# Softmax sums inverted by a GpSimd power, maximum taken by VectorE from a bfloat16 copy, and a new issue order, in a state-space and sliding-attention kernel

## Chip, cores and metric

One Trainium2 chip, one core. The metric is the device time of one execution in microseconds (us), the median of several runs of the same kernel. The engines are named as in the profile: PE (TensorE, matmuls; PEld its weight loads), DVE (VectorE), ACT (ScalarE), POOL (GpSimd) and SP (SyncE, which issues most DMAs).

## The reference

The inputs and the output are bfloat16. Part A is a diagonal state-space layer with L = 2048 steps, 448 channels and 448 complex states; part B is attention with 16 heads of 28, in which each position looks at 8 positions, 2 apart. Cut to what matters:

```python
# A
Lam_bar = exp(dt * Lam);  B_bar = ((Lam_bar - 1) / Lam)[:, None] * Bmat
h = Lam_bar * h + (x @ B_bar.T)[t]            # for each of 2048 steps
y = 2.0 * (h @ Cmat.T).real + x * Dskip
# B
q, k, v = split(x @ wqkv)                     # 16 heads of 28
logits[s, w] = (q[s] . k[s - 2 * w]) * scale  # w = 0..7; -1e9 where s - 2 * w < 0
attn = softmax(logits, axis=w)
o[s] = sum_w attn[s, w] * v[s - 2 * w]
b = o @ wo
out = concatenate([y, b], -1)                 # (1, 2048, 896)
```

The change is in the softmax of part B: the maximum over the 8 positions, the exponentials, their sum, and the product with the sum's reciprocal.

## The kernel before, in words

**Order.** Every piece of work is a unit of the `Planner` (L112), with an engine, a booked cost and dependences. The list `ORDER` (L51) holds all 685 unit numbers in the order in which they are issued; every engine executes its own in that order, so an instruction that waits holds up all behind it on its engine. What the units acquire and release (PSUM banks, the three `prods` buffers) fits that order.

**Part B.** The 2048 positions lie as 128 chunks on the partitions by 16 offsets, and the work is done in two halves of 8 offsets, b = 1 and then b = 0. For each half:

- `qk` (L584): DVE multiplies q with the shifted k (products `prods`, L654, L656, L660). PE sums them over the head's elements into the PSUM tile `logits`, 128 x 8 x 128 float32 (L672, L678). DVE can go on to the next product once one of three buffers is free.
- `softmax` (L695): PE adds the mask (L290); DVE takes the maximum over the 8 positions by a reduction out of PSUM (L701, `mx`); PE subtracts it (L705); ACT takes the exponentials (L711, `ex_sb`); PE sums the 8 positions into `sm_ps` (L716); DVE takes the reciprocal (L720, `rsum`) and multiplies (L722, `attn_t`); a transposing DMA that SP issues (L727) brings the result to `attn`.
- `v_proj` (L736): PE projects v (L753, L760), ACT evicts it (L218) into `vd`; POOL zeroes the halo (L778) and SP copies it (L773, L774).
- `pv` (L786): for each of the four groups of 4 offsets, DVE multiplies `attn` with v four times (L819, 128x3584 each) and adds three times (L822) and once over half the width (L838). In the last group the last add is made in two halves (L841). Three groups are transposed by a DMA (L872), the last by PE (L884); PE multiplies with wo (L900, L908, L915), ACT evicts, SP stores (L925).

**Part A** runs beside it. PE computes the inputs of the states (L1247) and the scan as products with tables of powers of `Lam_bar`, which DVE builds (L1197, `pw`, one for each of 7 blocks of states), with ACT evicting between the steps (L1263 to L1364). C is transposed by a DMA (L1024, `Ccat`), and the outputs are matmuls (L1458, L1462), evicted by ACT (L218) or, at the end, by DVE (L1474) and stored (L1477). `load_skip` (L1420) loads Dskip and A's x again for the last outputs, and DVE multiplies them (L1439).

Of the kernel before, what the change touches and what calls it, by code (L numbers as in the profile page):

```python
# [25 lines left out]
W = 8  # L26
# [13 lines left out]
NC = 3  # L40
# [6 lines left out]
ADD = (0, 0, 0, 0, 0, 0, 0)  # L47
EADD = (0, 0, 0, 0)
# [160 lines left out]
class Ctx:  # L209
# [111 lines left out]
class PartB:  # L321
# [373 lines left out]
    def softmax(self, b, prio):  # L695
        nc, pool, V, P, cx = self.nc, self.pool, self.nc.vector, self.plan, self.cx
        box = {}

        def top():
            box["mx"] = pool.tile([NCH, NCH], bf16, name="mx", tag="mx")  # L700
            V.tensor_reduce(box["mx"][:], self.lg[b][:].rearrange("p w q -> p q w"), axis=AX.X, op=ALU.max)  # L701
# [15 lines left out]

        def norm():
            r = pool.tile([NCH, 1, NCH], f32, name="rsum", tag="rs")
            V.reciprocal(r[:, 0, :], box["sm"][:])  # L720
            box["a"] = pool.tile([NCH, W, NCH], bf16, name="attn_t", tag="at_t")
            V.tensor_tensor(box["a"][:].rearrange("p w (c a) -> p w c a", c=2), box["e"][:].rearrange("p w (a c) -> p w c a", c=2),  # L722
                            r[:].rearrange("p o (a c) -> p o c a", c=2).to_broadcast([NCH, W, 2, 64]), op=ALU.mult)
# [5 lines left out]
        u = P.add("DVE", 1.23, top, [u], prio, acq="mx")  # L729
# [3 lines left out]
        u = P.add("DVE", 2.175, norm, [u], prio, rel=("s", "ex"), acq="at")  # L733
# [52 lines left out]
    def pv(self, b, prio, deps):  # L786
# [13 lines left out]
        lasts, halves, trs = {}, {}, {}  # L800
        for r in (1, 0):
            last = getattr(self, "pv_last", None)
            half = getattr(self, "u_half", None)
            ahead = half is not None
            us = (5, 4, 1, 0)
            for n in range(4):

                def step(n=n, r=r, part=0, half=half):
# [14 lines left out]
                    if n == 0:  # L823
                        mul(1 if half else 0)
                        mul(2 if half else 1)
                    elif n == 1 and half:
                        mul(3)
                        mul(0)
                    elif n == 2 and half:
                        add(1)  # L830
                        add(2)
# [3 lines left out]
                    elif 2 * b + r > 0:  # L835
                        add(3)
                        if not EADD[2 * b + r]:
                            V.tensor_tensor(acc[:, n1:2 * n1], acc[:, 0:n1], acc[:, n1:2 * n1], op=ALU.add)  # L838
# [4 lines left out]
                for u in us[:2 + ahead] if n == 0 else us[n + 1 + ahead:n + 2 + ahead] if n < 3 else ():  # L843
# [3 lines left out]
                cost = 2 * vec2(2 * n1) if n < 3 else vec2(2 * n1) + vec2(n1) * (not EADD[2 * b + r]) if 2 * b + r > 0 else vec2(n1)  # L847
                last = P.add("DVE", cost, step, dd + [self.u_attn[b], last, *self.u_prod[0], *self.u_prod[1], *self.u_lg[0], *self.u_lg[1],
                                         *self.u_vm, *self.u_proj, *deps, half if n == 1 else None], prio - 0.1 * r)
# [5 lines left out]
            g = 2 * b + r  # L855
            halves[g] = self.u_half = None
            if EADD[g]:

                def merge(g=g):
                    acc = self.acc[g]  # L860
                    nc.gpsimd.dma_start(acc[:, n1:2 * n1], acc[:, 0:n1], accum_op=ALU.add)
                halves[g] = self.u_half = P.add("POOL", 1.1, merge, [last], PRI["wo"], lat=3.5)
# [736 lines left out]
```

## Time and profile before

| | |
|---|---|
| median of 3 runs | 139.99 us (139.88 to 140.03) |
| the profiled execution's own time | 140.0 us |
| its span on the engines | 138.3 us |
| mean granted clock of PE | 0.997 |
| busy: PE, DVE | 131.3 us (95%), 123.0 us (89%) |
| busy: ACT, POOL | 88.3 us (64%), 17.7 us (13%) |
| the softmax's maximum on DVE (L701), 2 times | 1.22 us each |
| the reciprocal on DVE (L720), 2 times | 0.95 us each |
| the multiply behind it (L722), 2 times | 1.23 us each |

In a timeline a row holds the start in us, the duration in us, the engine, the line, the operation, the tiles (output <- inputs) with their shapes and types, and a count of instructions; in brackets stands how long the engine sat idle ahead of it and which instruction ended that. In a group, the numbers are the total busy time in us and the mean of one in ns. PE's matmuls are pipelined, so their durations overlap. L-numbers are lines of the kernel.

### The profile page before, as it was taken

The numbers are of one execution on the slowest core, as the hardware profiler recorded it, in microseconds if no ns is written. First come the engines' busy times: TensorE is split into PE (matmuls) and PEld (weight loads), VectorE is DVE, ScalarE is ACT, GpSimd is POOL, SyncE is SP. The second block draws the span as 40 slices with busy tenths as digits, with TensorE's granted clock in tenths as the row PEclk, the third lists the DMA queues.
The fourth block names the chain that finished last, engine by engine and source line by source line (L and its number), as shares of the span: only waits on it lengthen the run. The fifth ranks groups of instructions, "written<-read, shape, count | busy, mean of one in ns | idle before, by whom it ended". The sixth has DMA issues, their size and how long they took to land.

```text
span 138.3 us, 2835 instructions
## 1 busy us (share of the span) xinstructions
PE 131.3 (95%) x1065; PEld 67.2 (49%) x1071; DVE 123.0 (89%) x134; ACT 88.3 (64%) x199; POOL 17.7 (13%) x69
## 2 busy tenths in 40 slices
PE   7999989999999999999999999999999999999790
PEld 2534334444455453656534563556565455445450
DVE  1369998899999999997999999999999999999920
ACT  3555587998554976657695998689547151721571
POOL 7589830025000000000000000000000000000000
PEclk9999999999999999999999999999999999999998
DMA  4968965658658525648899039350093425575163
GB/s 128 269 126 208 179 87 61 153 130 95 81 113 53 97 52 112 179 104 131 167 222 198 0 67 240 95 111 0 0 95 103 139 78 118 141 163 169 35 197 100
DMA packets 41694, 16.58 MB, mean 120 GB/s; under 512 B 33685, under 2 KB 41044, under 8 KB 41681
## 3 DMA queue, kind: packets, MB, share of 16 engines
q1 hardware_dynamic: 41618, 16.40, 57.6%
q8 instruction: 8, 0.13, 0.4%
q14 instruction: 5, 0.04, 0.1%
q10 hardware_dynamic: 63, 0.01, 0.0%
HBM read 4.32 MB, written 3.67 MB: 58 GB/s over the span
## 4 chain that ended last, share of the span: by engine, by line
DVE 39%; PE 38%; SPq 9%; issue 5%; ACT 3%; DMA 3%; DVEq 0%; ACTq 0%
DVE rb L822 11%; DVE prods L819 11%; SPq L366 6%; PE v_ps L760 6%; PE scb L1247 5%; DVE rb L819 4%; PE scp L1247 4%; PE logits L672 3%; DMA rb<-in_B_x_dram 3%; DVE pw L1197 2%; PE qk_ps L481 2%; DVE prods L656 2%; PE wo_ps L915 2%; DVE rb L838 2%; ACT qk L218 1%
## 5 line engine op out<-in xcount | busy, mean ns | idle before, releaser
L819 DVE TENSOR_TENSOR prods<-attn,vd 128x3584 bf16<-128x3584 bf16 x12 | 24.0, 2018 | 0.0
L822 DVE TENSOR_TENSOR rb<-rb,prods 128x3584 bf16<-128x3584 bf16 x11 | 22.2, 2019 | 0.1
L656 DVE TENSOR_TENSOR prods<-qk 128x3072 bf16<-128x3072 bf16 (+1 forms) x15 | 19.1, 1325 | 0.0
L481 PE MATMUL qk_ps<-rb 128*128 128x512 bf16 x60 | 14.4, 379 | 0.7 <-DMA rb<-in_B_x_dram 0.6
L1462 PE MATMUL y_ps<-Ccat,qk 128*128 128x448 bf16 x60 | 14.6, 352 | 0.0
L218 ACT CAST vd<-v_ps 128x448 bf16<-128x448 f32 x16 | 7.9, 540 | 5.2 <-PE v_ps L760 4.9
L1247 PEld LDWEIGHTS <-Bcat 128*128 128x128 bf16 x84 | 7.5, 100 | 7.4 <-issue 1.1
L1294 ACT CAST ubuf<-scb 128x64 bf16<-128x64 f32 x35 | 7.3, 220 | 5.9 <-PE scb L1301 3.5
L218 ACT CAST qk<-wo_ps 128x448 bf16<-128x448 f32 (+1 forms) x16 | 8.1, 529 | 4.5 <-PE wo_ps L908 2.8
L1462 PE MATMUL y_ps<-Ccat,h 128*128 128x448 bf16 x45 | 11.0, 353 | 0.0
L1247 PE MATMUL scb<-xaT_sb,Bcat 128*128 128x512 bf16 x42 | 10.9, 380 | 0.0
L218 ACT CAST qk<-y_ps 128x448 bf16<-128x448 f32 (+1 forms) x9 | 5.6, 663 | 8.2 <-issue 4.2
L760 PE MATMUL v_ps<-rb 128*128 128x448 bf16 x48 | 10.1, 353 | 0.0
L220 ACT ACTIVATE qk<-qk_ps 64x512 bf16<-64x512 f32 (+1 forms) x15 | 8.9, 599 | 1.7 <-PE qk_ps L488 1.3
L481 PEld LDWEIGHTS <-rb 128*128 128x128 bf16 x60 | 5.6, 98 | 7.8 <-issue 1.0
L660 DVE TENSOR_TENSOR prods<-qk 128x768 bf16<-128x768 bf16 (+3 forms) x18 | 9.1, 566 | 0.1
L1462 PEld LDWEIGHTS <-qk 128*128 128x128 bf16 x60 | 5.8, 98 | 5.3 <-ACT qk L1364 0.2
L819 DVE TENSOR_TENSOR rb<-attn,vd 128x3584 bf16<-128x3584 bf16 x4 | 8.1, 2021 | 0.1
L908 PE MATMUL wo_ps<-wo_p,rb 128*128 128x448 bf16 x36 | 8.1, 353 | 0.0
L1197 DVE TENSOR_TENSOR pw<-Dm,spair 128x1920 bf16<-128x1920 bf16 x7 | 8.1, 1150 | 0.0
L218 ACT CAST qk<-qk_ps 128x512 bf16<-128x512 f32 (+2 forms) x11 | 6.3, 585 | 2.5 <-PE qk_ps L488 1.1
L1247 PE MATMUL scp<-xaT_sb,Bcat 128*128 128x512 bf16 x30 | 7.8, 381 | 0.0
(197 smaller groups left out, 259.0 us busy)
## 6 DMA issues: line engine op xcount, KB each, us to landing
out_dram<-qk SPq DMA_DIRECT2D x32, 112.0 KB, 1.8
vd<-vd SPq DMA_DIRECT2D x3, 392.0 KB, 4.5
rb<-in_B_wqkv_dram SPq DMA_DIRECT2D x3, 336.0 KB, 4.5
qk<-in_A_x_dram SPq DMA_DIRECT2D x1, 448.0 KB
ra<-in_A_B_re_dram SPq DMA_DIRECT2D x1, 392.0 KB, 4.3
ra<-in_A_B_im_dram SPq DMA_DIRECT2D x1, 392.0 KB
rb<-in_A_C_re_dram SPq DMA_DIRECT2D x4, 98.0 KB, 2.9
rb<-in_A_C_im_dram SPq DMA_DIRECT2D x4, 98.0 KB, 3.5
```

What stands on the lines that cost most here:

```text
L218: nc.scalar.copy(out, in_)
L220: nc.scalar.mul(out, in_, scale)
L366: nc.sync.dma_start(self.xT[:, j], bass.AP(x.tensor, x.offset + j * D - DT, [[T * D, NCH], [1, KT * NCH]]), transpose=True)
L481: nc.tensor.matmul(out(n), lhsT=w(n, full, k), rhs=self.xT[:, j:j + 4, k, :], start=(not rfirst and k == 1), stop=(rfirst and k == KT - 1) ...
L656: V.tensor_tensor(out.rearrange("p i j k q -> p i (j k) q"), qq.unsqueeze(1).to_broadcast([NCH, 2, 4 * nk, NCH]), bass.AP(kk.tensor, kk.of ...
L660: V.tensor_tensor(jk(out[:, i, a:e]), qq, kk, op=ALU.mult)
L760: nc.tensor.matmul(box["ps"][:].rearrange("p h d -> p (h d)"), lhsT=self.xT[:, j, k, :], rhs=self.wv[:, k, :], start=False, stop=(k == KT ...
L819: V.tensor_tensor(tmp[i].rearrange("p (j d h) -> p j d h", j=8, d=DH), aa, self.vd[:, o:o + 8], op=ALU.mult)
L822: V.tensor_tensor(acc, acc, tmp[i], op=ALU.add)
L1197: V.tensor_tensor(t[:], self.o["Dm"][:].rearrange("p (a b) -> p a b", b=2).unsqueeze(1).to_broadcast([NCH, 2 * NPW, 32, 2]), self.sp[:, m ...
L1247: mt(box[i], lhsT=self.Bcat[:, k, m, :], rhs=self.xk(slice(i, None, 4), k), start=(i % 2 == 0 and k == 0), stop=False, **kw)
L1462: nc.tensor.matmul(ps, lhsT=h, rhs=self.Ccat[:, m, :], start=(m == 0 and not skip), stop=(m == NM - 1), skip_group_check=True)
```

## The change

In each of the two softmaxes:

- ACT first copies the masked logits out of PSUM into a bfloat16 tile (`low`, L700 of the new kernel). DVE takes the maximum from it by three element-wise maxima over 4, 2 and 1 of the positions (L704, L705, L707: 512, 256 and 128 elements), in place of the one reduction out of PSUM.
- ACT copies the sums out of PSUM into `rsum` (`total`, L726); POOL raises them to the power -1 in place (`rec`, L730), with a tile of -1.0 that it sets at the start (L251) as the second operand; DVE does the multiply alone (L735). The bank of the sums is released by ACT's copy.

That is three more units in each half, 691 in all, and `ORDER` is a new list: through the first five numbers of its eighth row it is the old one with shifted numbers, behind them it is another order. What else the diff shows are options that were all zero, with their code.

```diff
+        self.minus = pool.tile([NCH, 1], f32, name="minus")
+        G.memset(self.minus[:], -1.0)
...
+        def low():
+            box["l"] = pool.tile([NCH, W, NCH], bf16, name="lg_bf", tag="lg_bf")
+            nc.scalar.copy(box["l"][:], self.lg[b][:])
+
         def top():
+            t = box["l"]
+            V.tensor_tensor(t[:, 0:4], t[:, 0:4], t[:, 4:8], op=ALU.max)
+            V.tensor_tensor(t[:, 0:2], t[:, 0:2], t[:, 2:4], op=ALU.max)
             box["mx"] = pool.tile([NCH, NCH], bf16, name="mx", tag="mx")
-            V.tensor_reduce(box["mx"][:], self.lg[b][:].rearrange("p w q -> p q w"), axis=AX.X, op=ALU.max)
+            V.tensor_tensor(box["mx"][:], t[:, 0], t[:, 1], op=ALU.max)
...
+        def total():
+            box["r"] = pool.tile([NCH, 1, NCH], f32, name="rsum", tag="rs")
+            nc.scalar.copy(box["r"][:, 0, :], box["sm"][:])
+
+        def rec():
+            r = box["r"][:, 0, :]
+            nc.gpsimd.tensor_tensor(r, r, cx.minus[:].to_broadcast([NCH, NCH]), op=ALU.pow)
+
         def norm():
-            r = pool.tile([NCH, 1, NCH], f32, name="rsum", tag="rs")
-            V.reciprocal(r[:, 0, :], box["sm"][:])
+            r = box["r"]
...
-        u = P.add("DVE", 1.23, top, [u], prio, acq="mx")
+        u = P.add("ACT", act(1024), low, [u], -1)
+        u = P.add("DVE", vec2(512) + vec2(256) + vec2(128), top, [u], prio, acq="mx")
...
-        u = P.add("DVE", 2.175, norm, [u], prio, rel=("s", "ex"), acq="at")
+        u = P.add("ACT", act(128), total, [u], -1, rel="s")
+        u = P.add("POOL", 2.0, rec, [u], -1)
+        u = P.add("DVE", 1.23, norm, [u], prio, rel="ex", acq="at")
```

DVE, from just ahead of the first softmax's reciprocal (b = 1) to the beginning of the weighted products, before (`prods<-qk` are products of q and k, `pw` is a table of powers, `rb<-attn,vd` the first weighted product):

```order
L656 TENSOR_TENSOR prods<-qk 128x3072
L720 RECIPROCAL rsum<-sm_ps 128x128
L722 TENSOR_TENSOR attn_t<-ex_sb,rsum 128x1024
L660 TENSOR_TENSOR prods<-qk 128x768 x2
L660 TENSOR_TENSOR prods<-qk 128x1536
L660 TENSOR_TENSOR prods<-qk 128x768 x2
L660 TENSOR_TENSOR prods<-qk 128x1536
L701 TENSOR_REDUCE mx<-logits 128x128
L819 TENSOR_TENSOR rb<-attn_1004,vd 128x3584
L819 TENSOR_TENSOR prods<-attn_1004,vd 128x3584
```

The same place in the new order:

```order
L655 TENSOR_TENSOR prods<-qk 128x3072
L659 TENSOR_TENSOR prods<-qk 128x256 x2
L659 TENSOR_TENSOR prods<-qk 128x512
L1196 TENSOR_TENSOR pw<-Dm,spair 128x1920
L735 TENSOR_TENSOR attn_t<-ex_sb,rsum 128x1024
L704 TENSOR_TENSOR lg_bf<-lg_bf 128x512
L705 TENSOR_TENSOR lg_bf<-lg_bf 128x256
L707 TENSOR_TENSOR mx<-lg_bf 128x128
L1196 TENSOR_TENSOR pw<-Dm,spair 128x1920
L833 TENSOR_TENSOR rb<-attn_1140,vd 128x3584
L833 TENSOR_TENSOR prods<-attn_1140,vd 128x3584 x2
```

The reciprocal is gone, the multiply (L735) stands behind all the products of q and k, and a second table of powers stands between the maximum and the weighted products; before, a table followed the first two of those.

DVE around the second softmax's multiply, which lies inside the second group of weighted products, before:

```order
L819 TENSOR_TENSOR prods<-attn_1004,vd 128x3584
L1197 TENSOR_TENSOR pw<-Dm,spair 128x1920
L720 RECIPROCAL rsum<-sm_ps 128x128
L722 TENSOR_TENSOR attn_t<-ex_sb,rsum 128x1024
L819 TENSOR_TENSOR prods<-attn_1004,vd 128x3584
L822 TENSOR_TENSOR rb<-rb,prods 128x3584
```

And in the new order, where it stands between two groups:

```order
L836 TENSOR_TENSOR rb<-rb,prods 128x3584 x2
L845 TENSOR_TENSOR rb<-rb 128x1792
L1196 TENSOR_TENSOR pw<-Dm,spair 128x1920
L735 TENSOR_TENSOR attn_t<-ex_sb,rsum 128x1024
L833 TENSOR_TENSOR rb<-attn_1140,vd 128x3584
```

The reciprocal is gone here too; the multiply now follows a table of powers behind a half add (L845).

POOL, from the zeroing of the scan's states (`S`) to its last instruction, before:

```order
L1212 MEMSET S 128x7x2
L402 MEMSET wo_p 64x448
L403 MEMSET wo_p 64x448
L778 MEMSET vd 1x896 x3
L778 MEMSET vd 1x448
```

And in the new order:

```order
L1211 MEMSET S 128x7x2
L794 MEMSET vd 1x896
L794 MEMSET vd 1x448
L730 TENSOR_TENSOR rsum<-rsum,minus 128x128
L401 MEMSET wo_p 64x448
L402 MEMSET wo_p 64x448
L794 MEMSET vd 1x896 x2
L730 TENSOR_TENSOR rsum<-rsum,minus 128x128
```

The two powers stand between the zeroings of v's halo (`vd`) and of the padding of wo (`wo_p`).

On SP the same transfers stand in another order: the transposition of C goes behind the second transposition of the weights, and the load of Dskip (L1429 before, L1410 now) moves from among the last stores to just ahead of the transposition of C.

More of the change, by code (lines that the diff above doesn't have):

```diff
@@ L39 @@
 NF = 3
-NC = 3
 WARM = 6
@@ L799, in pv, with step @@
         self.oTd = getattr(self, "oTd", {})
-        lasts, halves, trs = {}, {}, {}
+        lasts, trs = {}, {}
         for r in (1, 0):
             last = getattr(self, "pv_last", None)
-            half = getattr(self, "u_half", None)
-            ahead = half is not None
             us = (5, 4, 1, 0)
             for n in range(4):
-                def step(n=n, r=r, part=0, half=half):
+                def step(n=n, r=r, part=0):
                     alloc()
@@ L823, in step @@
                     if n == 0:
[L824 to L827, printed above, removed]
                         mul(0)
-                    elif n == 2 and half:
-                        add(1)
-                        add(2)
+                        mul(1)
                     elif n < 3:
@@ L836, in step @@
                         add(3)
[L837 to L838 removed]
+                        V.tensor_tensor(acc[:, n1:2 * n1], acc[:, 0:n1], acc[:, n1:2 * n1], op=ALU.add)
                     else:
@@ L842, in pv @@
                 dd = []
-                for u in us[:2 + ahead] if n == 0 else us[n + 1 + ahead:n + 2 + ahead] if n < 3 else ():
+                for u in us[:2] if n == 0 else us[n + 1:n + 2] if n < 3 else ():
                     o = j0 + 4 * r + DIL * u
@@ L846, in pv @@
                         dd += self.u_vh[p] if p < HALO else [self.u_v[p - HALO]]
-                cost = 2 * vec2(2 * n1) if n < 3 else vec2(2 * n1) + vec2(n1) * (not EADD[2 * b + r]) if 2 * b + r > 0 else vec2(n1)
+                cost = 2 * vec2(2 * n1) if n < 3 else vec2(2 * n1) + vec2(n1) if 2 * b + r > 0 else vec2(n1)
                 last = P.add("DVE", cost, step, dd + [self.u_attn[b], last, *self.u_prod[0], *self.u_prod[1], *self.u_lg[0], *self.u_lg[1],
-                                         *self.u_vm, *self.u_proj, *deps, half if n == 1 else None], prio - 0.1 * r)
+                                         *self.u_vm, *self.u_proj, *deps], prio - 0.1 * r)
             lasts[r] = [last, last]
@@ L854, in pv @@
             self.pv_last = last
[L855 to L862, printed above, removed]
             if not hasattr(self, "u_first"):
@@ L872, in trd @@
                     nc.sync.dma_start(t, self.acc[g][:, n1:2 * n1], transpose=True)
-                trs[r] = P.add("SP", 1.7, trd, [halves[g] or lasts[r][1]], PRI["wo"], lat=3.6)
+                trs[r] = P.add("SP", 1.7, trd, [lasts[r][1]], PRI["wo"], lat=3.6)
         for j in range(j0, j0 + JB):
@@ L1314, in ev3, with carry @@
                 nc.scalar.copy(hget()[:, 3, 0:384], box[3][:, 0:384])
-            def carry(out, lt, Sc, hv, new=False):
-                mt(out[:, 0:NCH], lhsT=lt, rhs=Sc, start=new, stop=True, **kw)
+            def carry(out, lt, Sc, hv):
+                mt(out[:, 0:NCH], lhsT=lt, rhs=Sc, start=False, stop=True, **kw)
                 mt(out[:, NCH:512], lhsT=lt, rhs=hv[:, 3, 0:384], start=False, stop=True, **kw)
@@ L1329, in ev1f, with back @@
                 nc.scalar.copy(hget()[:, 1, :], box[1])
-            def again(n, box=box, pair=pair):
+            def back(n, box=box, pair=pair, hget=hget):
                 if pair and n == 0:
@@ L1403, in scan @@
             b0 = b2 = eh
-            add = bool(ADD[m])
-            if not hold[0] and not add:
+            if not hold[0]:
                 b0 = P.add("PE", pe(1, 512), lambda f=back: f(0), [b0], PRI["bk"] + m * 0.1, acq="W" if pair else "s")
-            if not hold[pair ^ 1] and not add:
+            if not hold[pair ^ 1]:
                 b2 = P.add("PE", pe(1, 512), lambda f=back: f(1), [b2, b0], PRI["bk"] + m * 0.1, acq=None if pair else "s")
-            v0 = P.add("PE", pe(2, 256), s6, [b0, u3], pc, acq=("W" if pair else "s", "cP") if add else None)
-            v2 = P.add("PE", pe(1, 512), s7, [b2, u1, v0 if add and pair else None], pc, acq="s" if add and not pair else None)
+            v0 = P.add("PE", pe(2, 256), s6, [b0, u3], pc)
+            v2 = P.add("PE", pe(1, 512), s7, [b2, u1], pc)
             if pair:
@@ L1415, in scan @@
             done[m] = P.add("POOL", 0.0, lambda: None, [w0, w2, u1], rel=("fl", "pw"), lat=0.0)
-            if add:
-                w0 = w2 = P.add("POOL", 1.2, addin, [w0, w2], pc, rel="cP", lat=3.0)
             self.u_h.append((w0, u1, w2, [u3, eh]))
```

32 lines of the change are left out of this document (9 added, 23 removed), and 56 rows, old and new, of the table ORDER.

## The prediction

> **What bounds the kernel now.** I read first how busy the engines are in three stretches of the span: from the first maximum to the first weighted products, the long middle, and the end. The columns are the stretch, its length, then busy time and instructions of PE, PE's weight loads, DVE, ACT and POOL, and the granted clock.
>
> ```profile
> 44.00:65.00 21.00, 20.65 (x243) 11.23 (x243) 20.07 (x25) 14.86 (x36) 0.00 (x0) 1.00 0.56 108
> 65.00:127.00 62.00, 61.65 (x428) 32.79 (x431) 61.59 (x37) 39.38 (x100) 0.00 (x0) 1.00 0.53 119
> 127.00:138.30 11.30, 6.68 (x55) 3.77 (x53) 5.09 (x7) 4.99 (x10) 0.00 (x0) 0.96 0.32 102
> ```
>
> Two engines are full at once. From 44 to 127 us PE is busy 82.3 of 83 us and DVE 81.7. GpSimd does nothing after 44 us, and ScalarE has gaps. So work taken off DVE gains only as far as PE can be brought forward as well, while a delay on either moves the end at once, unless a wait swallows it.
>
> Next, the timeline of DVE through the first softmax (start, duration, instruction, and in brackets the idle time before it), and then through the second.
>
> ```profile
> 44.19 1.23 DVE L701 TENSOR_REDUCE mx<-logits 128x128 bf16<-128x1024 f32 x1
> 45.33 3.42 DVE L656 TENSOR_TENSOR prods<-qk 128x3072 bf16<-128x3072 bf16 x2
> ...
> 56.82 0.95 DVE L720 RECIPROCAL rsum<-sm_ps 128x128 f32<-128x128 f32 x1
> 57.87 1.23 DVE L722 TENSOR_TENSOR attn_t<-ex_sb,rsum 128x1024 bf16<-128x1024 bf16 x1
> 59.02 3.69 DVE L660 TENSOR_TENSOR prods<-qk 128x768 bf16<-128x768 bf16 x6
> 63.51 1.22 DVE L701 TENSOR_REDUCE mx<-logits 128x128 bf16<-128x1024 f32 x1 [0.80 <-PE logits L290]
> 64.65 2.02 DVE L819 TENSOR_TENSOR rb<-attn,vd 128x3584 bf16<-128x3584 bf16 x1
> ```
>
> ```profile
> 86.59 0.95 DVE L720 RECIPROCAL rsum<-sm_ps 128x128 f32<-128x128 f32 x1
> 87.64 1.23 DVE L722 TENSOR_TENSOR attn_t<-ex_sb,rsum 128x1024 bf16<-128x1024 bf16 x1
> 88.78 2.02 DVE L819 TENSOR_TENSOR prods<-attn,vd 128x3584 bf16<-128x3584 bf16 x1
> ```
>
> From start to start a maximum takes 1.14 and a reciprocal 1.05. In both softmaxes the reciprocal stands in an unbroken run of DVE. The only idle time here is the 0.80 before the second maximum, which waits for PE's mask. The attention-weighted products (L819) begin at 64.65, and from there DVE runs on to the halves of the last add.
>
> ```profile
> 126.48 2.09 DVE L841 TENSOR_TENSOR rb<-rb,prods 128x1792 bf16<-128x1792 bf16 x2
> 128.49 1.08 DVE L1439 TENSOR_TENSOR qk<-qk,rb 128x1792 bf16<-128x1792 bf16 x1
> ```
>
> ```profile
> 128.63 0.29 PE L884 MATMUL pt_o<-ident,rb 128*128 128x128 bf16 x2 [0.49 <-DVE rb L841]
> ...
> 130.46 0.92 PE L915 MATMUL wo_ps<-wo_p,rb 128*128 128x448 bf16 x4 [0.52 <-ACT qk L218]
> ...
> 131.98 0.61 PE L884 MATMUL pt_o<-ident,rb 128*128 128x128 bf16 x8 [0.17 <-DVE qk L1474]
> 132.43 2.43 PE L915 MATMUL wo_ps<-wo_p,rb 128*128 128x448 bf16 x12
> ```
>
> The add ends at 128.57, and the span 9.73 later, at 138.3. PE ends at 134.86; the 3.44 behind it are the last eviction, store and close. In the tail PE waits 0.49 + 0.52 + 0.17 = 1.18.
>
> **The maximum.** The reduction over PSUM goes; a ScalarE copy of the logits and three DVE maxima come. The nearest rows are ScalarE's copy of the same shape (and of 128x128, used further down), and DVE's two-input bf16 products of 256 and 512 elements.
>
> ```profile
> L1260 ACT CAST qk<-scP 128x1024 bf16<-128x1024 f32 x2 | 2.1, 1050 | 0.0
> ...
> L1287 ACT CAST eB<-scb 128x128 bf16<-128x128 f32 x7 | 2.0, 279 | 0.4 <-PE scb L1283 0.4
> ```
>
> ```profile
> L660 DVE TENSOR_TENSOR prods<-qk 128x256 bf16<-128x256 bf16 x4 | 1.0, 284 | 0.0
> L660 DVE TENSOR_TENSOR prods<-qk 128x512 bf16<-128x512 bf16 x2 | 0.8, 418 | 0.0
> ```
>
> The three, of 512, 256 and 128 elements, cost 0.42 + 0.28 + 0.21 (the slope between the two rows continued) = 0.91, and between 0.75, if their ends overlap, and 1.1, with a gap behind each; against 1.14 I take −0.25 per softmax. The price is the copy ahead of them, 1.05 and some 0.25 of hand-over, which stands between the mask and the maximum. Where it is hidden depends on when PE comes to the mask.
>
> ```profile
> 43.40 0.20 PE L290 MATMUL logits<-mrow,mcol 128*128 128x4 bf16 x2
> ...
> 63.27 0.21 PE L290 MATMUL logits<-mrow,mcol 128*128 128x4 bf16 x2
> ```
>
> ```profile
> L1247 PE MATMUL scb<-xaT_sb,Bcat 128*128 128x512 bf16 x42 | 10.9, 380 | 0.0
> L760 PE MATMUL v_ps<-rb 128*128 128x448 bf16 x48 | 10.1, 353 | 0.0
> ```
>
> Matmuls overlap: 512 columns follow each other every 0.216 us (0.81 for three, less the 0.38 of the last), 448 columns every 0.19. The new order has seven v matmuls fewer ahead of the first mask, −1.3, of which 0.3 to 0.5 are lost waiting for the sums: mask at about 42.6, copy done at 43.9, before DVE arrives at 44.16. No wait, so −0.25. Ahead of the second mask stand ten 512-column scan matmuls and eight small ones fewer, −1.9; less about 0.5 of waiting, the mask comes at 62.0, the copy is ready at 63.4, and the maxima last until 64.4.
>
> **The reciprocals leave DVE:** −1.05 each. Without any cost of the power, DVE's work from 45.33 to 62.71 (17.38) becomes 16.33 and starts 0.27 sooner: it ends at 61.4. But DVE then waits 2.1 for the copy, where it waited 0.80. The multiply now stands behind all products, and one more power table (L1197, pitch 1.07) stands ahead of the weighted products: 64.4 + 1.07 = 65.45. Before, with that table counted, they would have begun at 65.72. So of 1.6 freed, 0.27 is left at this place. Behind it the second reciprocal gives −1.05 in full, since DVE has no gap there, and a small cast that moved ahead −0.07. Sum so far: **−1.39**, DVE's end at 127.2.
>
> **The transposition of the weights** now starts at the multiply's end.
>
> ```profile
> attn<-attn_t SPq DMA_TRANSPOSE x2, 3.1
> ```
>
> That is 61.4 + 3.15 = 64.6 against 65.45: 0.85 of slack. Its cover is used up if the multiply comes 0.85 later.
>
> **The power.** Each softmax adds a ScalarE copy of 128x128 (0.28 by the row above) and a GpSimd operation, with two hand-overs, ahead of the multiply. No power is in the trace. GpSimd's two-input rows in float32 are these:
>
> ```profile
> L1124 POOL TENSOR_TENSOR cs<-sh 128x210 f32<-128x210 f32 x1 | 0.5, 539 | 0.0
> ...
> L1081 POOL TENSOR_TENSOR karg<-kv,arg 128x105 f32<-128x105 f32 x1 | 0.4, 362 | 0.0
> ```
>
> They give 1.69 ns an element, so 0.40 for 128: the lower bound, if a power costs what a product does. A logarithm, a product and an exponential make several such passes: five make 2.0, ten 4.0, the upper bound. I take 2.0, which is also what the code books for this unit; its bookings have been good where the trace can test them (1.23 for the maximum against 1.22; 2.175 for reciprocal and multiply against 0.95 + 1.23 = 2.18).
>
> Alone, that would be hidden. The first sums are finished on PE at about 57.5, their copy at 58.5, the power runs from 58.65 to 60.65, and the multiply is due at 60.25: it would come 0.4 to 0.6 late, which the 0.85 covers. In the second softmax the sums are finished more than 5 us ahead of the multiply. The question is whether GpSimd and DVE can read side by side at all.
>
> ```profile
> 14.80 1.08 POOL L1129 TENSOR_SCALAR la<-la,turn 128x7 f32<-128x7 f32 x1
> ```
>
> ```profile
> 14.68 0.96 DVE L654 TENSOR_TENSOR prods<-qk 128x1536 bf16<-128x1536 bf16 x1
> ```
>
> This is the one place in the trace where a reading GpSimd instruction meets a two-input product of DVE, and it bears against the change: an operation of 7 elements, whose twin took 0.50, took 1.08 and ended 0.23 after the product (15.64) that was under way when it began. One of them waits for the other. During both powers DVE runs two-input operations back to back, so if they exclude each other, DVE loses about the power's length: 2.0 and a hand-over.
>
> The Trainium skill, "SBUF — State Buffer", section "Who interferes with whom", has a rule for this: the two engines share one port pair under an exclusive lock, a VectorE operation with two SBUF inputs contends with GpSimd, and whoever starts first keeps the other out for its whole length. By that rule the sum is 141.6; without it, 139.1. The row above agrees with it in one short case, and no row shows a long GpSimd operation holding DVE up.
>
> With exclusion, the first multiply ends at 63.4 to 63.6 and not at 61.4, the weights land at 66.75, and the weighted products begin at 66.8 and not 65.45: +1.35. The second power stops an unbroken DVE: +2.1. With P as the power's length, the two cost about 2P − 0.6.
>
> **What else is moved.** POOL gets one small memset at the start, and the zeroings of the halo are moved about the powers; it is idle after 44 us otherwise. On SP the transposition of C (Ccat) and the load of Dskip go behind the second transposition of the weights.
>
> ```profile
> 70.49 4.08 SPq L1024 DMA_TRANSPOSE Ccat<-rb  x1
> ```
>
> ```profile
> L1462 PE MATMUL y_ps<-Ccat,h x45: 352/353/353, 96.1 to 126.0; 128*128 128x448 bf16 x45
> ```
>
> The second multiply stands 15.7 of DVE's work behind the first weighted product, at 81.15 without the power and some 3.45 later with it, so it ends near 86; the transposition behind it is issued by 87.5 and Ccat by 91.6, so that it lands at 93 to 94. Its first reader stood at 96.1, and by PE's pitches stands near 96.8 in the new order: I cost this at nothing, with some 3 us of cover; a power of 4 us would use it up. PE has the same rows in another order; I cost that order at nothing in the middle, since PE was full in it before, and at 0.3 where PE itself would set the end.
>
> **The sum.** DVE: −1.39 + 1.35 + 2.1 = +2.06, so its add ends at 130.6. The tail behind it, 9.73 before, now holds 32 transposing matmuls at 0.056 (eight from 131.98 to 132.43) and 26 of 448 columns at 0.19, which is 6.75, and the 3.44 at the end. It begins 0.15 behind the first half of the add, 1.05 ahead of the second's end: 0.15 + 6.75 + 3.44 − 1.05 = 9.3, so −0.4, if PE doesn't wait in it. Span 138.3 + 2.06 − 0.4 = 139.95. The profiled execution took 140.0 for its span of 138.3, and 140.0 is also the median of the runs (139.99), so I add 1.7: **141.6 us**.
>
> **Rivals.**
>
> 1. *The power costs DVE little*: no exclusion for long operations, or a power below 0.8 us. For it: no row shows DVE held up by GpSimd. Against it: L1129. DVE's end moves to 127.2 or a little later and PE becomes the bound: it gives up the 1.18 of tail waits and pays about 0.3 for more changes between kinds of matmul. Span 137.4, **139.1 us**, faster than before. It decides at 2P − 0.6 = 1.39 + 0.4, a power of 1.2 us.
> 2. *Break-even*: a power of 1.0 to 1.4 us with exclusion, or a long one without it whose late multiply just moves the products: 139.7 to 140.3.
> 3. *A long power*, up to 4.0 with exclusion: 2P − 0.6 is 7.4, 4.0 more than the forecast's 3.4: about **145.6**. For it: ten passes are not excluded by any row. Against it: the booking.
> 4. *The change does not free DVE*: the instruction lists show that both reciprocals are off DVE, so this is only the waits of rival 2 or 3.
>
> **How the numbers follow.** Forecast (140.6 to 143.5, a power of 1.5 to 2.9 with exclusion): 0.50. Rival 1: 0.33. Rival 2: 0.08. Rival 3: 0.09. A measurement of this kernel tells about 0.2% from no change, 139.7 to 140.3. Faster 0.33, same 0.08, slower 0.50 + 0.09 = 0.59. The range reaches into rival 1 to 138.7 and into rival 3 to 144.2; the forecast's own is 140.6 to 143.5.
>
> **What would show it.** Right: two GpSimd rows of about 2 us at 58 to 61 and 75 to 79; beside them a DVE operation about 2 us longer than its kind; weighted products from about 66.8; the last add's end near 130.6. Wrong: DVE's rows beside the power at their old durations (then rival 1), power rows near 0.4 or near 4 us, or the first mask so late that the maximum waits for the copy. A DVE end below 128.6 with a later span would mean that the new order of PE or the stores costs what I put at nothing.

## The result, and the profile after

The changed kernel takes 175.23 us (median of 4 runs, 174.32 to 176.16), against 139.95 for the kernel before in the same session: a ratio of 1.2521 (95% interval 1.2449 to 1.2593). The profiled execution has a span of 173.1 us and took 174.8. The forecast was 141.6, the range 138.7 to 144.2: the direction was right, the size wrong by 33.6 us.

First the page of the changed kernel: PE, POOL and PE's granted clock in 40 slices of the span (tenths), and its two groups with the longest idle time on their engine.

```profile
PE   8999999999999970001999999600799999968992
...
POOL 7588100200000599998000999980000000000000
PEclk9999999999999998555799999985599999996999
...
L730 POOL TENSOR_TENSOR rsum<-rsum,minus 128x128 f32<-128x128 f32 x2 | 41.8, 20878 | 40.1 <-ACT rsum L726 26.8
L735 DVE TENSOR_TENSOR attn_t<-ex_sb,rsum 128x1024 bf16<-128x1024 bf16 x2 | 2.5, 1226 | 34.9 <-POOL rsum L730 34.9
```

The slices show two holes on PE that were not there before. POOL is full through the first and ahead of the second, and through the first part of it. The group says what fills POOL: two powers of 20.9 us each. Behind them DVE's multiply has waited 34.9 us. The timeline of POOL, then DVE's around both multiplies and at its last add:

```profile
58.32 20.81 POOL L730 TENSOR_TENSOR rsum<-rsum,minus 128x128 f32<-128x128 f32 x1 [26.82 <-ACT rsum L726]
...
95.07 20.95 POOL L730 TENSOR_TENSOR rsum<-rsum,minus 128x128 f32<-128x128 f32 x1 [13.32 <-issue]
```

```profile
58.44 1.03 DVE L659 TENSOR_TENSOR prods<-qk 128x256 bf16<-128x256 bf16 x3
59.39 1.15 DVE L1196 TENSOR_TENSOR pw<-Dm,spair 128x1920 bf16<-128x1920 bf16 x1
79.16 1.23 DVE L735 TENSOR_TENSOR attn_t<-ex_sb,rsum 128x1024 bf16<-128x1024 bf16 x1 [18.63 <-POOL rsum L730]
...
83.72 2.02 DVE L833 TENSOR_TENSOR rb<-attn,vd 128x3584 bf16<-128x3584 bf16 x1 [1.35 <-DMA attn<-attn_t]
...
116.05 1.23 DVE L735 TENSOR_TENSOR attn_t<-ex_sb,rsum 128x1024 bf16<-128x1024 bf16 x1 [16.28 <-POOL rsum L730]
...
159.83 2.10 DVE L848 TENSOR_TENSOR rb<-rb,prods 128x1792 bf16<-128x1792 bf16 x2
```

Two things are to be seen. The multiply starts 0.03 us behind the power's end, both times: nothing else is waited for. And DVE's two-input rows beside the power keep their length but for 0.2 us once (1.15 for the table of powers, as before; the three small products 1.03 where they take 0.82 elsewhere). So the power doesn't hold DVE off its data; DVE has nothing to do, because the next instruction in its queue needs the reciprocal. The last add ends at 161.93, and at 128.57 before.

PE waits with it. The second maximum stands behind the first multiply on DVE, and PE's subtraction behind that maximum. The second hole goes on past the power's end at 116.02: there PE waits for a table of powers (L1196) that stands behind the second multiply and two weighted products on DVE.

```profile
81.36 1.01 PE L711 MATMUL logits<-mx,nident 128*128 128x512 bf16 x2 [17.36 <-DVE mx L707]
...
122.27 0.61 PE L1265 MATMUL scb<-qk,pw 128*128 128x512 bf16 x1 [11.20 <-DVE pw L1196]
```

### The profile page after: what moved, and what is told of

Its sections match the earlier page's. It is cut to its first block, busy times and chain, and to the rows that moved or that the text cites. A ratio compares the mean times of both kernels' runs of the same rounds, so it can differ in the third digit from the quotient of the medians.

```text
span 173.1 us, 2848 instructions
## 1 busy us (share of the span) xinstructions
PE 137.6 (79%) x1071; PEld 68.9 (40%) x1071; DVE 121.3 (70%) x136; ACT 91.4 (53%) x203; POOL 59.5 (34%) x72
## 4 chain that ended last, share of the span: by engine, by line
DVE 19%; PE 17%; POOLq 12%; POOL 12%; issue 10%; SPq 2%; DMA 2%; ACT 1%; ACTq 0%
POOLq L1575 12%; POOL rsum L730 12%; DVE rb L836 7%; DVE prods L833 6%; PE v_ps L776 2%; DVE rb L833 2%; PE y_ps L1443 2%; DMA out_dram<-qk 2%; PE wo_ps L907 2%; PE wo_ps L914 2%; PE scp L1246 2%; PE logits L671 2%; DVE rb L845 1%; PE pt_o L883 1%; SPq L871 1%
## 5 line engine op out<-in xcount | busy, mean ns | idle before, releaser
L730 POOL TENSOR_TENSOR rsum<-rsum,minus 128x128 f32<-128x128 f32 x2 | 41.8, 20878 | 40.1 <-ACT rsum L726 26.8
L735 DVE TENSOR_TENSOR attn_t<-ex_sb,rsum 128x1024 bf16<-128x1024 bf16 x2 | 2.5, 1226 | 34.9 <-POOL rsum L730 34.9
L711 PE MATMUL logits<-mx,nident 128*128 128x512 bf16 x4 | 1.6, 496 | 17.4 <-DVE mx L707 17.4
L1443 PE MATMUL y_ps<-Ccat,qk 128*128 128x448 bf16 x60 | 14.3, 352 | 0.0
L1265 PE MATMUL scb<-qk,pw 128*128 128x512 bf16 x8 | 3.5, 444 | 11.2 <-DVE pw L1196 11.2
L1246 PE MATMUL scb<-xaT_sb,Bcat 128*128 128x512 bf16 x42 | 12.0, 401 | 0.0
L717 ACT ACTIVATE ex_sb<-logits 128x1024 bf16<-128x1024 f32 x2 | 2.0, 1024 | 17.8 <-DVE pw L1196 17.8
L1443 PE MATMUL y_ps<-Ccat,h 128*128 128x448 bf16 x45 | 11.0, 353 | 0.0
L1269 ACT CAST e<-scb 128x512 bf16<-128x512 f32 x7 | 4.1, 587 | 12.3 <-PE scb L1265 11.9
L1293 ACT CAST ubuf<-scb 128x64 bf16<-128x64 f32 x35 | 7.0, 217 | 5.1 <-PE scb L1300 2.3
L907 PE MATMUL wo_ps<-wo_p,rb 128*128 128x448 bf16 x36 | 9.5, 395 | 0.0
```

The lines of the kernel that those rows point to most:

```text
L730: nc.gpsimd.tensor_tensor(r, r, cx.minus[:].to_broadcast([NCH, NCH]), op=ALU.pow)
L907: nc.tensor.matmul(ps[:], lhsT=self.oTd[g][:, a + kt], rhs=self.wo_p[:, 5 * e + kt, :], start=False, stop=(kt == 2), skip_group_check=True)
L1246: mt(box[i], lhsT=self.Bcat[:, k, m, :], rhs=self.xk(slice(i, None, 4), k), start=(i % 2 == 0 and k == 0), stop=False, **kw)
L1443: nc.tensor.matmul(ps, lhsT=h, rhs=self.Ccat[:, m, :], start=(m == 0 and not skip), stop=(m == NM - 1), skip_group_check=True)
```

## The experiments

Times are medians; a ratio stands against runs of the kernel before on the same chip. A time without a ratio is that of a single run.

**1. One product in place of the power.** The reciprocal is left out; everything else of the change stays.

```diff
-            nc.gpsimd.tensor_tensor(r, r, cx.minus[:].to_broadcast([NCH, NCH]), op=ALU.pow)
+            nc.gpsimd.tensor_tensor(r, r, cx.minus[:].to_broadcast([NCH, NCH]), op=ALU.mult)
```

> The changed kernel with a product in place of the power, same operands, same place (the reciprocal is left out, so the weights are not normalized). Theory 1: the GpSimd operation takes about 0.4 us, the multiply no longer waits, time 138.8 to 139.6 us. Rival (something else in the chain copy, GpSimd, multiply is slow, such as the start of a GpSimd operation behind a semaphore): GpSimd rows of 0.4 but the multiply still waits several us, time over 142 us.

Measured: 138.89 us, 0.9915 (0.9897 to 0.9933), a span of 137.2. POOL's first product and the DVE rows that answer to those above:

```profile
58.51 0.46 POOL L730 TENSOR_TENSOR rsum<-rsum,minus 128x128 f32<-128x128 f32 x1 [26.83 <-ACT rsum L726]
```

```profile
60.65 1.22 DVE L735 TENSOR_TENSOR attn_t<-ex_sb,rsum 128x1024 bf16<-128x1024 bf16 x1
63.09 0.43 DVE L704 TENSOR_TENSOR lg_bf<-lg_bf 128x512 bf16<-128x512 bf16 x1 [1.23 <-ACT lg_bf L700]
...
65.20 2.02 DVE L833 TENSOR_TENSOR rb<-attn,vd 128x3584 bf16<-128x3584 bf16 x1
...
81.14 1.22 DVE L735 TENSOR_TENSOR attn_t<-ex_sb,rsum 128x1024 bf16<-128x1024 bf16 x1
...
124.92 2.09 DVE L848 TENSOR_TENSOR rb<-rb,prods 128x1792 bf16<-128x1792 bf16 x2
```

Neither multiply waits. So the chain of ScalarE's copy, a GpSimd instruction and the multiply costs nothing by itself; the operation alone makes the difference between 138.9 and 175.2. The accounts of the two traces close: the add ends at 127.01 here and at 161.93 with the power, 34.9 later; that is 34.9 of waits for the power and 1.35 for the landing of the weights, less the 1.23 of the second maximum's wait, which is covered there: 35.0, so 0.1 is left open. The spans differ by 35.9; the last 1.0 is the tail, which PE sets (11.2 from the add's end against 10.2). With the power, PE stops once more for 2.23 us shortly ahead of the tail, for an eviction of ScalarE, which itself had waited for a store. Its last group of the outputs (L1443) before the transposing matmuls then begins 1.7 us ahead of the add's end, where it begins 2.7 ahead with one product. Behind the stop PE works at half its clock for some 3 us (last section). That stop and clock make the 1.0 is read from the traces; no run tests it.

```profile
155.80 0.53 ACT L215 CAST qk<-wo_ps 128x448 bf16<-128x448 f32 x1 [6.45 <-DMA out_dram<-qk]
156.38 0.96 PE L899 MATMUL wo_ps<-wo_p,rb 64*128 64x448 bf16 x2 [2.23 <-ACT qk L215]
```

**2. The reciprocal back on VectorE**, all else as changed:

```diff
-            nc.gpsimd.tensor_tensor(r, r, cx.minus[:].to_broadcast([NCH, NCH]), op=ALU.pow)
...
+            V.reciprocal(r[:, 0, :], r[:, 0, :])
```

> The changed kernel with the power undone alone: ScalarE still copies the sums, but VectorE takes the reciprocal from that copy, as before the change, ahead of its multiply. New maximum and new order stay. Theory 1 (the power's own length, 20.9 us twice, is the whole loss): the waits of 18.6 and 16.3 us are gone and VectorE pays two reciprocals of about 0.95, the first partly inside the 2 us that it waits for the second maximum's copy; the last add ends near 128.4, time 139.0 to 140.0 us. Rival (the new order costs by itself, through PE or the y buffers in the tail, where the changed kernel was 1.4 us longer): 141 us or more.

Measured: 140.36 us, 1.002 (1.0008 to 1.0033), so a little over the expected band. The first reciprocal and the first weighted product on DVE:

```profile
60.40 0.95 DVE L733 RECIPROCAL rsum<-rsum 128x128 f32<-128x128 f32 x1
...
65.92 2.02 DVE L833 TENSOR_TENSOR rb<-attn,vd 128x3584 bf16<-128x3584 bf16 x1 [0.67 <-DMA attn<-attn_t]
```

The loss of 35 us is gone, so it was the power's. New maximum and new order together bring nothing while DVE still makes the reciprocal: the late multiply makes DVE wait 0.67 for the weights to land, and the add ends at 128.64, where it ended at 128.57 before.

**3. Half the power** (64 of 128 columns; the other sums are not inverted):

```diff
-            nc.gpsimd.tensor_tensor(r, r, cx.minus[:].to_broadcast([NCH, NCH]), op=ALU.pow)
+            nc.gpsimd.tensor_tensor(r[:, 0:64], r[:, 0:64], cx.minus[:].to_broadcast([NCH, 64]), op=ALU.pow)
```

> The power over 64 of the 128 columns; the other sums are not inverted. If the power's cost is by element: rows of about 10.5 us and a time some 20 us shorter than the changed kernel's, 154 to 156 us. If most of it is a fixed start: rows near 20 us and a time near 174 us.

```profile
58.53 10.62 POOL L730 TENSOR_TENSOR rsum<-rsum,minus 128x64 f32<-128x64 f32 x1 [26.82 <-ACT rsum L726]
```

156.85 us, 0.85 over the expected band; the second power, which began inside a DVE operation, took 11.60. From 10.62 to 20.81 for 64 columns more is 159 ns a column, and on a straight line 0.43 is left as a start, which is about what a whole product took (0.46). Two lengths can't test the line itself. But nearly all of the power's time goes with its columns, not with a start or a first use: in no run is the second power shorter than the first by more than 0.03.

**4. Another exponent**, 2.0 for −1.0 (the weights are multiplied by the squares of the sums):

```diff
-        G.memset(self.minus[:], -1.0)
+        G.memset(self.minus[:], 2.0)
```

> The changed kernel with exponent 2.0 in place of -1.0 (the weights are multiplied by the square of the sums). If the power is computed in the same way whatever the exponent: rows of 20.8 us and about 175 us. If the time depends on the value (a special case for small whole exponents): rows clearly shorter.

177.33 us in one run, with powers of 20.81 and 22.15. The first is as long as with −1.0 to a hundredth, so 2.0 takes no shorter way. (The second is 1.2 longer than with −1.0; the next two experiments show waits of that kind.)

**5. Five products**, some 2 us of GpSimd work, which is what the forecast assumed (the reciprocal is left out):

```diff
-            nc.gpsimd.tensor_tensor(r, r, cx.minus[:].to_broadcast([NCH, NCH]), op=ALU.pow)
+            for _ in range(5):
+                nc.gpsimd.tensor_tensor(r, r, cx.minus[:].to_broadcast([NCH, NCH]), op=ALU.mult)
```

> Five products in a row in place of the power, about 2.0 us of reading GpSimd work beside VectorE's two-input products: the length that the forecast assumed (the reciprocal is left out). Exclusion of the two engines: VectorE's rows beside them are longer by about 2 us in sum, or the five products stretch to the length of VectorE's run; time 141 to 142 us. No exclusion: GpSimd's five rows stay near 0.4 each, VectorE's rows keep their durations, time 139.0 to 139.8 us.

Measured: 141.19 us, 1.0066 (1.0046 to 1.0087), 2.3 more than with one product, and within the band for exclusion. The five in the second softmax on POOL, and what DVE did meanwhile:

```profile
76.34 2.11 POOL L731 TENSOR_TENSOR rsum<-rsum,minus 128x128 f32<-128x128 f32 x1 [11.82 <-issue]
78.53 2.06 POOL L731 TENSOR_TENSOR rsum<-rsum,minus 128x128 f32<-128x128 f32 x1
80.67 1.13 POOL L731 TENSOR_TENSOR rsum<-rsum,minus 128x128 f32<-128x128 f32 x1
81.88 1.19 POOL L731 TENSOR_TENSOR rsum<-rsum,minus 128x128 f32<-128x128 f32 x1
83.15 0.40 POOL L731 TENSOR_TENSOR rsum<-rsum,minus 128x128 f32<-128x128 f32 x1
```

```profile
76.17 2.02 DVE L837 TENSOR_TENSOR rb<-rb,prods 128x3584 bf16<-128x3584 bf16 x1
78.23 2.10 DVE L837 TENSOR_TENSOR rb<-rb,prods 128x3584 bf16<-128x3584 bf16 x1
80.36 1.17 DVE L846 TENSOR_TENSOR rb<-rb 128x1792 bf16<-128x1792 bf16 x1
81.46 1.35 DVE L1197 TENSOR_TENSOR pw<-Dm,spair 128x1920 bf16<-128x1920 bf16 x1
83.58 1.23 DVE L736 TENSOR_TENSOR attn_t<-ex_sb,rsum 128x1024 bf16<-128x1024 bf16 x1 [0.77 <-POOL rsum L731]
```

A product that takes 0.40 on a free machine lasts here until 0.26 behind the end of the DVE operation under way: 78.45 against 78.19, 80.59 against 80.33, 81.80 against 81.53, 83.07 against 82.81. The exclusion is there, but it is GpSimd that pays: it gets one instruction into each change between two DVE operations, and each of these turns costs DVE 0.08 to 0.2 (2.10 for 2.02, 1.17 for 1.09, 1.35 for 1.15). In the second softmax the five products become 7.2 us, and then the multiply has to wait for the last of them (0.77, in both softmaxes).

**6. A power that nobody waits for.** Both reciprocals are on DVE, as in experiment 2, and in the second softmax GpSimd raises a spare copy of the sums, which nothing reads:

```diff
+            if b == 0:
+                box["z"] = pool.tile([NCH, NCH], f32, name="spare", tag="spare")
+                nc.scalar.copy(box["z"][:], box["sm"][:])
...
+                nc.gpsimd.tensor_tensor(box["z"][:], box["z"][:], cx.minus[:].to_broadcast([NCH, NCH]), op=ALU.pow)
```

> The changed kernel with both reciprocals on VectorE (the 140.4 us kernel), and beside it, in the second softmax only, a power of 128x128 on a spare copy of the sums that nothing reads. It starts near 76 us and runs beside some twelve two-input operations of VectorE without a gap. If a power held VectorE off for its length (exclusion over the whole instruction), VectorE's add would end about 20 us later: 155 to 161 us. If the power only waits for its turn and then runs by itself, VectorE's rows grow by 0.1 to 0.2 each time a turn is taken, once or twice: 140.4 to 141.0 us, and the power takes 21 to 23 us. If it needs many turns, its row is much longer than 23 us.

Measured: 140.58 us, 1.0032 (1.0014 to 1.0051); the same as experiment 2 within the intervals. The power, and two rows of DVE, which did not stop beside it, at its start and inside it:

```profile
76.55 21.81 POOL L733 TENSOR_TENSOR spare<-spare,minus 128x128 f32<-128x128 f32 x1 [42.19 <-ACT spare L729]
```

```profile
75.73 4.16 DVE L840 TENSOR_TENSOR rb<-rb,prods 128x3584 bf16<-128x3584 bf16 x2
...
94.87 4.08 DVE L840 TENSOR_TENSOR rb<-rb,prods 128x3584 bf16<-128x3584 bf16 x2
```

The power is 1.1 longer than one that met DVE idle (20.75, in experiment 9); it began 1.2 us ahead of the end of a DVE operation, at 77.8. DVE loses 0.08 once (4.16 for 4.08); all later rows have their usual length. So a 21.8 us GpSimd instruction does not hold DVE off. The Trainium skill, "SBUF — State Buffer", section "Who interferes with whom", says that whoever comes first has the shared pair for the whole instruction. For short products that fits the rows of experiment 5 on GpSimd's side; for the power it doesn't, and the measurement decides: DVE ran its two-input operations all through it.

**7. The new maximum alone, in the old order:**

```diff
-            V.tensor_reduce(box["mx"][:], self.lg[b][:].rearrange("p w q -> p q w"), axis=AX.X, op=ALU.max)
+            t = pool.tile([NCH, W, NCH], bf16, name="lg_bf", tag="lg_bf")
+            nc.scalar.copy(t[:], self.lg[b][:])
+            V.tensor_tensor(t[:, 0:4], t[:, 0:4], t[:, 4:8], op=ALU.max)
+            V.tensor_tensor(t[:, 0:2], t[:, 0:2], t[:, 2:4], op=ALU.max)
+            V.tensor_tensor(box["mx"][:], t[:, 0], t[:, 1], op=ALU.max)
```

> The kernel before with the new maximum alone (ScalarE's copy, three VectorE maxima), in the old order. Theory (the copy stands on the path wherever PE comes to the mask just ahead of VectorE): the first maximum waits 0.75 us for the copy, the second 2.1 in place of 0.80, each maximum saves 0.25; VectorE loses 0.5 + 1.05, time 141.2 to 141.8 us. Rival (the copy is hidden, the maxima gain their 0.25 each): 139.4 to 139.8 us.

Measured: 141.37 us, 1.0101 (1.0079 to 1.0124), as expected. Both maxima wait for the copy:

```profile
44.60 0.42 DVE L702 TENSOR_TENSOR lg_bf<-lg_bf 128x512 bf16<-128x512 bf16 x1 [0.53 <-ACT lg_bf L701]
...
64.82 0.42 DVE L702 TENSOR_TENSOR lg_bf<-lg_bf 128x512 bf16<-128x512 bf16 x1 [1.78 <-ACT lg_bf L701]
```

The three maxima save about 0.2 on DVE (0.92 from start to start for the first, 1.14 before). The copy puts 1.1 us between the mask and the maximum (the masks end at 43.51 and 63.73), which becomes waiting wherever PE comes to the mask just ahead of DVE. So the new maximum pays only in an order that has the mask earlier.

**8. The old maximum in the new order**, the reciprocal on DVE (only the order, and ScalarE's small copy, are new):

```diff
-            nc.scalar.copy(box["l"][:], self.lg[b][:])
...
+            V.tensor_reduce(box["mx"][:], self.lg[b][:].rearrange("p w q -> p q w"), axis=AX.X, op=ALU.max)
```

> The changed kernel with the reciprocal on VectorE and the old reduction as the maximum, so that only the order is new (beside ScalarE's small copy of the sums). Against the kernel with the reciprocal on VectorE and the new maximum (140.36): the first maximum costs 0.25 more, the second is hidden behind the landing of the weights either way, so 140.4 to 140.7 us. Rival (the new maximum costs more than it saves even in the new order): 139.9 or less.

140.66 us, 1.0046 (1.0026 to 1.0067), against 1.002 (1.0008 to 1.0033) with the new maximum. The difference is of the size expected, but the intervals overlap, so it is suggested and not shown.

**9. The power alone, in the old order**, twice. First copy and power stood where the reciprocal had stood:

```diff
-            V.reciprocal(r[:, 0, :], box["sm"][:])
+            nc.scalar.copy(r[:, 0, :], box["sm"][:])
+            nc.gpsimd.tensor_tensor(r[:, 0, :], r[:, 0, :], cx.minus[:].to_broadcast([NCH, NCH]), op=ALU.pow)
```

> The kernel before with the power alone (ScalarE's copy, GpSimd's power of 128x128), in the old order and with the old maximum. The power is 20.9 us long and its sums are ready 0.3 and 4.6 us ahead of the multiply: VectorE waits about 21.3 and 16.5 us and saves two reciprocals; 174 to 178 us. If the new order had been hiding part of the power or had been costing part of the loss, this comes out by that much over or under the changed kernel's 175.2.

It took 186.26 us, a miss, but not for the reason given: at that place in its queue ScalarE came to the copy 2.9 and 7.1 us behind the end of the sums (59.62 against 56.74, and 113.73 against 106.64; the next expectation has 3.0 and 6.7). So it was run again with the same two lines moved behind the matmuls of the sums:

> The kernel before with the power alone, as in the run that took 186.3 us, but with ScalarE's copy of the sums and the power issued right behind the matmuls of the sums (there the copy stood 3.0 and 6.7 us behind them). Waits of about 21 and 16.5 us at the multiplies: 174 to 178 us, which would say that the new order hides nothing of the power. If 180 or more, the new order does hide some of it.

179.3 us, between the two expected bands. The waits of the multiply, there and in the changed kernel (in all, times, longest):

```profile
DVE attn_t L726 <- POOL rsum L721: 40.3, 2, 21.0
```

```profile
DVE attn_t L735 <- POOL rsum L730: 34.9, 2, 18.6
```

The power is as long (20.75 and 21.92). The new order hides 5.4 us more of it, by the products that now stand ahead of the first multiply and the half add and table ahead of the second, and the whole change is 4 us better than the power alone. Each of the two times with the old order is of one run, so these 4 us are a rough figure. No more is hidden in this order, since what follows a multiply in DVE's queue stays behind it.

**10. The reciprocal on ScalarE**, as the exponential of minus the logarithm:

```diff
-            nc.scalar.copy(box["r"][:, 0, :], box["sm"][:])
+            nc.scalar.activation(box["r"][:, 0, :], box["sm"][:], ACT.Ln)
+            nc.scalar.activation(box["r"][:, 0, :], box["r"][:, 0, :], ACT.Exp, scale=-1.0)
...
-            nc.gpsimd.tensor_tensor(r, r, cx.minus[:].to_broadcast([NCH, NCH]), op=ALU.pow)
```

> The changed kernel with the reciprocal made by ScalarE as the exponential of minus the logarithm, out of the sums' bank, in place of copy and power. If ScalarE can do it beside the scan, the multiply starts near 60.7 and 81.2 and the time is that of the kernel with one product on GpSimd, 138.9 us. If the logarithm needs tables of its own (1.28 us for a load in the kernel before, two to four more of them), the first multiply comes 1 to 2 us late and the scan's evictions with it: 139.5 to 142 us.

147.29 us, 1.0487 (1.044 to 1.0534): worse than expected. Each of the four functions loads a table first. This is the group of the two logarithms' loads, one in each softmax (that of the exponentials' reads the same):

```profile
L726 ACT ACT_TABLE_LOAD x2 | 2.6, 1283 | 0.0
```

So each softmax puts two loads, 2.6 us, into ScalarE's queue (3.2 us from 58.89 to 62.09 with the two functions), while PE waits for its evictions: 5.1 us in three waits for `ubuf` (L1293). Then with one table set that holds both functions, loaded once:

```diff
+            if b == 1:
+                nc.scalar.preload_act_table_set("natural_log_exp_and_others")
             nc.scalar.activation(box["e"][:], self.lg[b][:], ACT.Exp)
```

> The changed kernel with the reciprocal made by ScalarE as the exponential of minus the logarithm, as in the run of 147.3 us, but with one table set that holds both functions, loaded once ahead of the first exponential of the softmax in place of its own load; the four later loads are gone. ScalarE then spends 0.59 us for each reciprocal in place of the copy's 0.28. If the loads were the cost there: the first multiply starts near 60.7 and the second near 81.2 without waiting, time 138.7 to 139.3 us, faster than both kernels and the same as with one product on GpSimd (138.89). If ScalarE's queue itself is too full there: 140 us or more, with waits of PE for ScalarE's evictions.

Measured: **138.99 us, 0.991 (0.9885 to 0.9935)**: 0.9% less than the kernel before, a small gain but clear of the noise, and far below the changed kernel. ScalarE's two functions, and DVE's first multiply:

```profile
58.24 0.28 ACT L728 ACTIVATE rsum<-sm_ps 128x128 f32<-128x128 f32 x1
58.55 0.31 ACT L729 ACTIVATE rsum<-rsum 128x128 f32<-128x128 f32 x1
```

```profile
60.51 1.22 DVE L737 TENSOR_TENSOR attn_t<-ex_sb,rsum 128x1024 bf16<-128x1024 bf16 x1
```

The reciprocal is ready at 58.9, 1.6 ahead of its multiply, and the rest runs as with one product on GpSimd. The Trainium skill, "ScalarE: Activation LUTs", section "Table sets: the hidden batching unit", names this set as the one with both functions; the traces agree. They have 1.28 us for a load, and no idle time beside it, where that section counts about 2.7.

## Why the prediction was wrong

- **The power: the step that failed.** It was bounded by 0.40 and 4.0 us, and 2.0 taken; it took 20.81 and 20.95. The upper end was worked out from passes of 0.4, but no row or run shows how a power is made, or in how many passes; the kernel's own booking of 2.0 was trusted because other bookings agreed with rows, but those were of operations that the kernel before had run, and this one it had not. One product in its place (138.89) and the reciprocal back on DVE (140.36) show that this price alone is the loss; half the power shows that it goes with the columns.
- **The hiding of it** (0.85 of slack ahead of the weighted products) failed with the price. The forecast had the first power start at 58.65 (58.32) and the multiply follow at once. With 20.9 put into its own order of work, and nothing for exclusion, the weighted products begin at 58.65 + 20.9 + 1.15 + 3.15 = 83.85 (measured 83.72), 18.4 late; the second power, whose sums the forecast has ready more than 5 us ahead, at about 75.7, then runs from 75.7 + 18.4 to 115.0, 15.5 behind its due time; DVE's add ends at 128.57 − 1.39 + 18.4 + 15.5 = 161.1 (161.93). So what waits for what was right. The forecast's own formula for a longer power was not: 2P − 0.6, with 20.9, is 41.2 and puts the add's end at 168.4, since it has DVE stand still for both powers.
- **Exclusion** was right for products and wrong for the power, and wrong in who pays. The forecast had DVE lose the power's whole length. Five products cost DVE 0.08 to 0.2 a turn and GpSimd up to 1.7 each; a power cost DVE 0.08 in experiment 6 and 0.2 at the first softmax of the changed kernel. That five products came out at 141.2, near the forecast of 141.6, is in part another way to the same time: DVE waited 0.77 twice for a GpSimd that had been held up.
- **Rival 1** was wrong for the change itself, which is slower by a quarter, but its sum for everything but the power was right: forecast 139.1 and a span of 137.4, measured 138.89 and 137.2 with one product, 138.99 and 137.4 with ScalarE's reciprocal. In detail: DVE's add 127.2 (127.01), weighted products 65.45 (65.20), second multiply 81.15 (81.14), masks 42.6 and 62.0 (42.7 and 61.8), first maximum without a wait (so). The tail was forecast 0.4 shorter than before and was 0.5 longer, since PE set the end there, as that rival had it.
- **The maximum**: −0.25 where the copy is hidden was nearly right (−0.22: 0.92 from start to start in experiment 2, 1.14 before). The copy does stand on the path where it is not hidden (experiment 7), at 1.1 and not 1.3.
- **Rivals 2 and 3.** A long power (rival 3) was the right doubt, with an upper bound five times too small and with an exclusion that the power does not show. A long power without exclusion, whose late multiply moves the products, stood in rival 2 only, and there at 140. No rival had a power over 4.0 us or a time over 145.6, so what happened had no chance of its own.

The trace before spoke against that price of exclusion already. L1129 was not the only meeting of the two engines in it: at 8.93 a small DVE operation with two inputs began inside a reading GpSimd instruction and was over in 0.17, while the other went on to 9.25. So DVE was not held for that one's length.

```profile
8.75 0.50 POOL L1091 TENSOR_SCALAR kc<-kf 128x105 f32<-128x105 f32 x1
```

```profile
8.93 0.17 DVE L1114 TENSOR_TENSOR ll<-pf,rden 128x14 f32<-128x14 f32 x1
```

Open: whether ScalarE's reciprocal would gain as much in the old order; it was not run. Why a power takes 159 ns a column is not shown either, only that it does so whatever the exponent tried.

## What to carry to other kernels

An operation that no row of the trace shows has no upper bound from the rows of other operations; if the next instruction of a full engine waits for it, the chance of a price ten times higher belongs into the range, whatever the code books for it. One run with that operation in it would have told. To free an engine of an operation, look first for an engine whose price for it is known and whose queue has room just there: 0.59 us on ScalarE did what 20.9 us on GpSimd could not.

## What was not expected of the hardware

- GpSimd's power of 128x128 float32 took 20.8 us where DVE hardly met it, some 159 ns a column, against 0.46 for a product with the same operands.
- GpSimd's reading instructions get in between two two-input operations of DVE, and end 0.26 behind the one that was under way (experiment 5); DVE pays 0.08 to 0.2 for each. A power of 21.8 us waited once, about 1.1 us, and then ran beside DVE (experiment 6).
- PE's granted clock falls in a hole. Stretches of the changed kernel, each with its length, PE's busy time and instructions, the clock, and then the DMA engines' busy share and GB/s:

```profile
61.00:79.00 18.00, 3.00 (x37) 0.69 0.00 0
79.00:82.00 3.00, 0.64 (x2) 0.50 0.12 24
82.00:85.00 3.00, 3.00 (x10) 0.54 0.94 234
85.00:90.00 5.00, 5.00 (x35) 1.00 0.92 171
```

After 17.4 us without a matmul PE comes back at 0.50 and has its full clock again some 3 to 4 us later; ten matmuls filled the 3 us from 82 to 85. DVE's rows there keep their length. The stop of 2.23 us ahead of the tail had the same effect: 0.50 from 157 to 159.5, and 1.00 from 160.
